# Cosformer attention and a mixture of experts: scaling k by cos and v by tan, kv with t innermost, row writes on VectorE, expert weights later

## The chip, the cores and the metric

The kernel runs on one core of one Trainium2 chip. The time is device microseconds for one execution, the median of several runs. A core has TensorE (PE, matmuls; its weight loads are listed as PEld), VectorE (DVE), ScalarE (ACT), GpSimd (POOL) and SyncE (SP, which here only issues transfers). Sixteen DMA engines move data between HBM and the on-chip memories SBUF and PSUM. The profile is of one execution and is somewhat longer than the timed runs.

## The reference

Eight batches of eight heads, 576 tokens, head dimension 64, go through a linear attention with a cosine weighting; its output, 4608 rows of 512, goes to one of eight experts each (top 1).

```python
theta = np.pi / 2.0 * pos / S                       # S = 576
phi(x) = concat([relu(x) * cos(theta), relu(x) * sin(theta)], -1)
kv  = einsum('bhsf,bhsd->bhfd', phi(k), v)          # f = 128, d = 64
z   = sum_s phi(k)
num = einsum('bhsf,bhfd->bhsd', phi(q), kv)
den = einsum('bhsf,bhf->bhs', phi(q), z) + 1e-06
x   = (num / den) as 4608 rows of 512
# experts
logits = x @ w_gate                                 # 8 experts
e = argmax(logits); g = softmax(logits)[e]          # denominator + 1e-9
# a token keeps its place if its expert has fewer than 1152 tokens before it
out[i] = g[i] * (relu(x[i] @ w1[e]) @ w2[e])        # 512 -> 1024 -> 512
```

The kernel never builds phi(q). Because sin = cos * tan, the query side is num = relu(q) kv_cos + tan * relu(q) kv_sin, and the common factor cos of a row falls out between num and den (den's 1e-6 is divided by cos for it).

## The kernel before

A list of operations is written with a cost, a priority and what it reads and writes; a small scheduler in the kernel file orders them on the host, and each engine then runs its instructions in that order. Tiles come from rings ("slots"): `p` and `a` are PSUM buffers (three and two), the rest lies in SBUF.

Attention of one batch `b`. The two halves `u` are four heads each; `j` counts nine tokens per partition, `t` is cos or sin:

```python
kS, vS, qS = Slots("km", 4), Slots("vm", 2), Slots("qm", 2)
vsS, rqS, kvaS = Slots("vs", 2), Slots("rq", 2), Slots("kva", 2)
tmpS = Slots("tmp", 3)

def relu_k(u):                                     # ACT; DVE for b == 0
    nc.scalar.activation(out=kk, in_=kk, func=ACT.Relu)        # 128 x 1152
def scale_v(j, t, us):                             # j odd or 4: ACT, else DVE
    tab = (cosn, sinn)[t]
    dst, src = vs_t[vs.slot][:, heads, j, t, 0:D], vm.tile[:, heads, j, :]
    # ACT: activation(Copy, scale=tab[:, j:j+1]);  DVE: tensor_scalar(mult)
# ...
def kv_half(u):                                    # PE: per j, c, o
    nc.tensor.matmul(out=kv_v[c * D:(c + 1) * D, o, u, :, :],
                     lhsT=loaded[b, "k", u].tile[o * D:(o + 1) * D, c, j, :],
                     rhs=vs_t[vs.slot][o * D:(o + 1) * D, 2 * u + c, j, :, :], ...)
def kvt_out():   # ACT copy of kv without z, to be transposed for the gate logits
def kva_out():   # ACT copy of kv with z
# T: four transposes of kvt; G: times w_gate; g_out: logits columns beside kv in kva

def p_unit(c, u, pv, tmp):                         # ten units a batch
    # PE:  p = relu(q)^T (as weights) x kva, cos and sin part side by side
    # ACT: tmp = p[cos part]
    nc.scalar.copy(out=t[0:rows], in_=p_v[0:rows, :, 0:KW])
    # DVE: num = p[sin part] * tan + tmp
    nc.vector.scalar_tensor_tensor(out=num..., in0=p_v[0:rows, :, KW:2 * KW],
        scalar=tant[0:rows, c:c + 1], in1=tmp.tile[0:rows], op0=ALU.mult, op1=ALU.add)
```

Routing of a batch follows: a chain of small DVE instructions gives the expert, the gate and the place of each token. Then the rows are scaled, written as bf16 (`xg`, five pieces) and scattered to a DRAM buffer `xd` sorted by expert:

```python
ON_POOL = (1, 3)
def f_emit(c):
    eng = nc.gpsimd if c in ON_POOL else nc.vector
    eng.tensor_tensor(out=x[0:rows, c, 0:DT]..., in0=num.tile[0:rows, c, :, 0:D],
                      in1=rv["rden"][0:rows, c, :]...to_broadcast(...), op=ALU.mult)
def f_scat(c):                                     # GpSimd queue
    nc.gpsimd.indirect_dma_start(out=xd[:, :], ...)
```

After the rows of six batches are in `xd`, 43 blocks of 128 rows are fetched and go through the experts: transpose, `up` with w1 (two halves w1a and w1b), relu, transpose, `down` with w2, indirect store. All expert weights are loaded with a cast to bf16 on the GpSimd queue; w1a during attention, w1b and w2 after it:

```python
for e in range(E):
    w1_load(0, e, e + 0.1, ops_of("KV", 3 * e // 4))   # after KV of batch 0, 0, 1, 2, 3, 3, 4, 5
for e in range(E):
    w1_load(1, e, 50.0 + e, [swapped])                 # after attention
```

## Time and profile before

Three runs took 385.45, 386.87 and 390.52 us, median 386.87. The profiled execution spans 396.6 us at a mean granted TensorE clock of 0.932.

| engine | busy us | share of the span | instructions |
|---|---|---|---|
| PE (matmul) | 336.3 | 85% | 3368 |
| PEld (weight loads, beside PE) | 221.2 | 56% | 3368 |
| DVE | 210.2 | 53% | 584 |
| ACT | 188.9 | 48% | 403 |
| POOL | 154.3 | 39% | 214 |

Some groups that the change touches:

| line, operation | engine | count | mean ns |
|---|---|---|---|
| L419 relu of k, 128x1152 | ACT | 14 | 1169 |
| L433 scaling of v, 128x256 | ACT | 70 | 519 |
| L435 scaling of v, 128x256 | DVE | 56 | 340 |
| L516 and L521 copies of kv | ACT | 16 | 571 and 605 |
| L581 tmp, 128x292 | ACT | 64 | 403 |
| L586 num, 128x292 | DVE | 64 | 517 |
| L758 row write, 128x512 | DVE | 16 | 1115 |
| L758 row write, 128x512 | POOL | 16 | 1520 |

How the lines are read. "L586" is line 586 of the kernel. A group of instructions gives line, engine, operation, output and input names, count, then busy time in us and the mean ns of one, then the idle time of the engine just before them and what ended it. A stretch ("70.00:90.00 20.00, ...") gives its length, then the busy us of PE, PEld, DVE, ACT and POOL with counts, the granted clock, the mean share of the 16 DMA engines that was busy, and GB/s. The slices of the page are 40 equal parts of the span, each digit a busy share in tenths. In the chain of waits each piece is start us, length us, and the work or transfer that the end depended on there. In the order of instructions the bracket gives the idle time in front and who ended it. Matmuls of fp32 count twice.

### The profile page before, as it was taken

The page shows a single profiled execution, that of the slowest core. Times are in us where ns is not written, and L with a number is a line of the kernel's source. Part 1 is how long each engine was busy: PE and PEld are TensorE (multiplying, and loading weights), DVE is VectorE, ACT ScalarE, POOL GpSimd, SP SyncE. Part 2 cuts the span into 40 slices and gives each one's busy share as a digit, 9 for nine tenths or more (in the row PEclk, how much of TensorE's full clock was granted, in tenths as well). Part 3 has the DMA queues.
Part 4 walks back from the last instruction along what each step waited for, and adds up shares of the span by engine and source line. Part 5 has one row for each costly group of instructions (what it writes and reads, how often), then busy time and mean ns, then how long its engine had stood idle before and what let it go on. Part 6 is the DMA issues. An engine that isn't in the chain of part 4 may idle for free.

```text
span 396.6 us, 9673 instructions
## 1 busy us (share of the span) xinstructions
PE 336.3 (85%) x3368; PEld 221.2 (56%) x3368; DVE 210.2 (53%) x584; ACT 188.9 (48%) x403; POOL 154.3 (39%) x214
## 2 busy tenths in 40 slices
PE   6588698878897996788397787899999999999992
PEld 3477597757686875674254343455555544444440
DVE  6547878796867697878725333444333311222220
ACT  5576776777675695547063232345555311111110
POOL 6100546454653627084723222105000065555552
PEclk9978986999797799989879998999999999999998
DMA  8999787778979501126599997819920033342330
GB/s 271 335 341 311 246 248 225 240 223 260 259 221 229 197 3 62 45 71 147 172 202 236 202 213 146 176 47 165 211 51 2 1 134 159 139 162 110 126 129 1
DMA packets 38543, 66.63 MB, mean 168 GB/s; under 512 B 3903, under 2 KB 18655, under 8 KB 38498
## 3 DMA queue, kind: packets, MB, share of 16 engines
q0 software_dynamic: 18096, 31.00, 34.5%
q1 hardware_dynamic: 19250, 33.98, 26.1%
q10 hardware_dynamic: 1152, 1.05, 0.8%
q8 instruction: 29, 0.48, 0.5%
q14 instruction: 16, 0.13, 0.1%
HBM read 67.56 MB, written 17.06 MB: 213 GB/s over the span
## 4 chain that ended last, share of the span: by engine, by line
PE 44%; DVE 15%; DMA 12%; issue 11%; POOL 6%; ACT 5%; POOLq 2%; ACTq 2%; SPq 1%; DVEq 0%
PE p L999 17%; PE p L574 9%; PE p L1040 7%; POOL out_dram L1057 6%; DMA xr<-xd 5%; DMA vm<-in_v_dram 5%; PE a L1014 4%; DVE xg L758 4%; DVE num L586 3%; PE a L468 3%; DMA qm<-in_q_dram 2%; POOLq L1057 2%; ACT tmp L581 2%; PE a L976 2%; PE a L547 1%
## 5 line engine op out<-in xcount | busy, mean ns | idle before, releaser
L1006 ACT ACTIVATE h<-p 128x512 bf16<-128x512 f32 x86 | 51.3, 598 | 63.3 <-PE p L999 61.7
L1040 PE MATMUL p<-w,un 128*128 x344 | 74.6, 379 | 0.3 <-issue 0.3
L574 PE MATMUL p<-kva,rq 64*128 64x146 f32 x640 | 61.2, 345 | 13.9 <-DVE num L586 10.9
L1020 DVE COPY un<-a 128x512 bf16<-128x512 bf16 x86 | 36.0, 423 | 63.5 <-PE a L1014 63.3
L574 PEld LDWEIGHTS p<-kva,rq 64*128 64x128 f32 x640 | 53.1, 229 | 21.8 <-DVE num L586 14.5
L1040 PEld LDWEIGHTS <-un 128*128 128x128 bf16 x344 | 33.6, 98 | 40.6 <-issue 0.6
L586 DVE SCALAR_TENSOR_TENSOR num<-p,tant,tmp 128x292 f32<-128x292 f32 (+1 forms) x80 | 39.8, 516 | 24.4 <-ACT tmp L581 19.2
L767 POOL DMA_INDIRECT xd<-xg,si x40 | 47.1, 1178 | 11.1 <-issue 8.8
L999 PEld LDWEIGHTS <-un 128*128 128x128 bf16 x344 | 32.7, 99 | 30.5 <-issue 9.5
L999 PE MATMUL p<-w1a,un 128*128 x172 | 46.7, 399 | 2.5 <-POOL ids L971 0.5
L581 ACT COPY tmp<-p 128x292 f32<-128x292 f32 (+1 forms) x80 | 31.2, 402 | 35.3 <-PE p L574 25.8
L1048 DVE COPY y<-p 128x512 f32<-128x512 f32 x22 | 15.2, 691 | 57.7 <-PE p L1040 51.9
L999 PE MATMUL p<-w1b,un 128*128 x172 | 44.1, 378 | 0.0
L1057 POOL DMA_INDIRECT out_dram<-y,ids x20 | 19.5, 976 | 58.5 <-DVE y L1048 46.8
L504 PE MATMUL p<-vs,km 64*64 64x130 f32 x1152 | 34.6, 272 | 9.1 <-DVE km L421 4.3
L1046 ACT COPY y<-p 128x512 f32<-128x512 f32 x21 | 12.3, 586 | 61.2 <-PE p L1040 61.2
L504 PEld LDWEIGHTS p<-vs,km 64*64 64x64 f32 x1152 | 32.1, 133 | 11.2 <-issue 5.2
L1014 PEld LDWEIGHTS <-h 128*128 128x128 bf16 x344 | 25.2, 99 | 22.5 <-ACT h L1006 10.0
L1014 PE MATMUL a<-identb,h 128*128 128x128 bf16 x344 | 33.5, 222 | 4.9 <-ACT h L1006 4.2
L758 POOL TENSOR_TENSOR xg<-num,rden 128x512 bf16<-128x512 f32 x16 | 24.0, 1520 | 18.4 <-DVE rden L735 18.4
L971 POOL COPY ids<-xr 128x2 bf16<-128x2 bf16 x43 | 7.6, 190 | 56.6 <-DMA xr<-xd 56.3
L468 PE MATMUL a<-ident,qr 128*128 128x128 f32 x144 | 27.3, 319 | 2.1 <-ACT rq L475 1.8
(162 smaller groups left out, 405.2 us busy)
## 6 DMA issues: line engine op xcount, KB each, us to landing
vm<-in_v_dram SPq DMA_DIRECT2D x16, 576.0 KB
km<-in_k_dram SPq DMA_DIRECT2D x16, 576.0 KB
qm<-in_q_dram SPq DMA_DIRECT2D x16, 576.0 KB
w<-in_moe_w_dram POOLq DMA_DIRECT2D x16, 512.0 KB
xr<-xd SPq DMA_DIRECT2D x43, 128.5 KB
w1a<-in_moe_w_dram POOLq DMA_DIRECT2D x8, 512.0 KB
w1b<-in_moe_w_dram POOLq DMA_DIRECT2D x8, 512.0 KB
xd<-zrow ACTq DMA_DIRECT2D x8, 128.5 KB
```

Source lines behind the costliest of these rows:

```text
L468: nc.tensor.transpose(out=q_ps[:, n * P:(n + 1) * P], in_=qr.tile[:, j, :, :].rearrange("p c d -> p (c d)"), identity=ident[:])
L504: nc.tensor.matmul(out=kv_v[c * D:(c + 1) * D, o, u, :, :], lhsT=loaded[b, "k", u].tile[o * D:(o + 1) * D, c, j, :], rhs=vs_t[vs.slot][o * ...
L574: nc.tensor.matmul(out=p_ps[:, a, o, 0:2 * KW], lhsT=rq[u].tile[a * D:(a + 1) * D, o, col:col + P], rhs=kva.tile[a * D:(a + 1) * D, o, u, ...
L581: nc.scalar.copy(out=t[0:rows], in_=p_v[0:rows, :, 0:KW])
L586: nc.vector.scalar_tensor_tensor(out=num.tile[0:rows, c, u * HB:(u + 1) * HB, :], in0=p_v[0:rows, :, KW:2 * KW], scalar=tant[0:rows, c:c + ...
L758: eng.tensor_tensor(out=x[0:rows, c, 0:DT].rearrange("p (h d) -> p h d", h=H), in0=num.tile[0:rows, c, :, 0:D], in1=rv["rden"][0:rows, c, ...
L767: si = nc.gpsimd.indirect_dma_start(out=xd[:, :], out_offset=bass.IndirectOffsetOnAxis(ap=xg.si[0:rows, c:c + 1], axis=0), in_=xg.tile[0:r ...
L999: nc.tensor.matmul(out=hp, lhsT=xv.tile[:, g, :], rhs=w1h[m][:, bass.ds(e1, 1), g, :], start=(g == 0), stop=(g == G - 1))
L1006: nc.scalar.activation(out=h[:], in_=pvs[m].tile[:, 0, :].rearrange("p (g q i) -> p g i q", g=2, i=2), func=ACT.Relu)
L1014: nc.tensor.transpose(out=t_ps[:, x * P:(x + 1) * P], in_=hvs[m].tile[:, x // 2, x % 2, :], identity=identb[:])
L1040: nc.tensor.matmul(out=y_ps, lhsT=hts[x // G].tile[:, x % G, :], rhs=w2h[x // G][:, bass.ds(e2, 1), x % G, :], start=(x == 0), stop=(x == ...
L1057: oi = nc.gpsimd.indirect_dma_start(out=out[:, :], out_offset=bass.IndirectOffsetOnAxis(ap=idx, axis=0), in_=yv.tile[:], in_offset=None, b ...
```

## The change

- The scalings change sides. k becomes relu(k)*cos in one instruction per j, and v*tan is added beside the untouched v, so that a KV matmul with relu(k)*cos on the left has v (cos part) and v*tan (sin part) on the right. v and v*tan of a slot lie in one tile and are joined by one operand with a stride between two runs of 66 elements. The `vs` tiles and the relu of k alone go away.
- kv is stored with t innermost (cos and sin of an element side by side), so one copy serves both the transposes and the p matmuls; kvt goes away. p comes out with t innermost too, and tmp and num read every second element.
- Row writes go to VectorE alone, in the order of the pieces. In routing the product for the gate logits is written with heads innermost and summed contiguously; the 1e-9 of the softmax is a ninth column, which takes an instruction on GpSimd away.
- w1a is loaded after KV of batches 4 to 7 (two loads each).
- Many evacuations may go to ACT or DVE, as the scheduler finds free; priorities (PHI) and ring sizes are set anew: km 2 slots of a whole batch, qm 4, rq 3, tmp 4.

It is meant to take work off ACT and DVE in attention, to keep GpSimd and VectorE out of each other's way, and to leave the first microseconds of DMA to q, k and v.

```diff
-    kS, vS, qS = Slots("km", 4), Slots("vm", 2), Slots("qm", 2)
-    vsS, rqS, kvaS = Slots("vs", 2), Slots("rq", 2), Slots("kva", 2)
-    tmpS = Slots("tmp", 3)
+    kS, vS, qS = Slots("km", 2), Slots("vm", 2), Slots("qm", 4)
+    rqS, kvaS = Slots("rq", 3), Slots("kva", 2)
+    tmpS = Slots("tmp", 4)
# ... scalings
+        def scale_k(j, us):
+            def f(eng):
+                kk = km.tile[:, 2 * us[0]:2 * us[-1] + 2, j, :]
+                if eng == "ACT":
+                    nc.scalar.activation(out=kk, in_=kk, func=ACT.Relu, scale=cosn[:, j:j + 1])
+                else:
+                    nc.vector.tensor_scalar(out=kk, in0=kk, scalar1=0.0, scalar2=cosn[:, j:j + 1], op0=ALU.max,
+                                            op1=ALU.mult)
+        def scale_v(j, us):
+            def f(eng):
+                dst, src = v_tan(vm.slot)[:, heads, j, 0:D], v_raw(vm.slot)[:, heads, j * D:(j + 1) * D]
+                # ACT: activation(Copy, scale=tann[:, j:j+1]);  DVE: tensor_scalar(mult)
# ... KV: columns 0:66 of v at (h, j) and of v*tan at (h, j)
+                            both = bass.AP(first.tensor, first.offset, [tuple(first.ap[0]), (v1 - v0, 2), (1, VX)])
+                            nc.tensor.matmul(out=kv_v[c * D:(c + 1) * D, 2 * o + u, :, :],
+                                             lhsT=km.tile[rows, 2 * u + c, j, :], rhs=both,
# ... one copy of kv, t innermost
+            t = tl(kva, [P, 4, KW, 2], FP32, "early")
+            copy(out=t[:, :, 0:D, :].rearrange("p w d t -> p w t d"), in_=kv_tile()[:, :, :, 0:D])
+            copy(out=t[:, :, D, :], in_=kv_tile()[:, :, 1, D:D + 2])
# ... evacuation of p
-                nc.scalar.copy(out=t[0:rows], in_=p_v[0:rows, :, 0:KW])
+                (nc.scalar.copy if eng == "ACT" else nc.vector.tensor_copy)(out=t[0:rows], in_=by_t(0))
-                    ... in0=p_v[0:rows, :, KW:2 * KW],
+                    ... in0=by_t(1),
# ... row writes
-                eng = nc.gpsimd if c in ON_POOL else nc.vector
-                eng.tensor_tensor(
+                nc.vector.tensor_tensor(
# ... weights
-        w1_load(0, e, e + 0.1, ops_of("KV", 3 * e // 4))
+        w1_load(0, e, e + 0.1, ops_of("KV", min(4 + e // 2, B - 1)))
```

Cut here: the scheduler's part that lets an operation choose between two engines, the set-up of the tables (tan on all partitions, the spread of w_gate on VectorE), and the same choice of engine for rq, tsb, gout, xT, relu, hT and y.

## The prediction

> **What bounds the kernel now.** I read the forty slices of the page first, for stages; then the busy times stretch by stage; then the chain of waits in order of time; then the instructions in order of time of one attention batch; last the groups of instructions by line and shape, for the durations used below.

> ```profile
> PE   6588698878897996788397787899999999999992
> DVE  6547878796867697878725333444333311222220
> ACT  5576776777675695547063232345555311111110
> DMA  8999787778979501126599997819920033342330
> ...
> 70.00:90.00 20.00, 16.25 (x283) 13.59 (x279) 16.46 (x43) 15.03 (x36) 10.55 (x10) 1.00 0.76 225
> 180.00:200.00 20.00, 12.78 (x94) 7.13 (x94) 15.68 (x53) 9.13 (x19) 12.08 (x20) 0.89 0.66 160
> 200.00:220.00 20.00, 17.82 (x142) 10.59 (x140) 7.99 (x21) 8.61 (x16) 5.10 (x13) 0.93 1.16 229
> 265.00:314.00 49.00, 48.70 (x349) 27.16 (x347) 19.13 (x47) 25.50 (x43) 5.63 (x8) 1.00 0.47 87
> ```

> A slice is 9.9 us. Three stages show. Attention runs to about 178 us: PE, DVE and ACT are each seven to nine tenths busy and none is full (70 to 90 us: PE 16.3, DVE 16.5, ACT 15.0 of 20 us at full clock), so the order and the waits between them set the pace. From 178 to about 250 us the experts start while DMA is full (1.16 from 200 to 220 us). From 265 us on PE is full (48.7 of 49) up to the last blocks; nothing on ACT or DVE can shorten that.

> ```profile
> 11.99 18.04 DMA vm<-in_v_dram
> ...
> 84.04 2.99 DVE xg L758 x2
> 87.03 0.67 DVE qr L458
> 87.97 1.30 DVE num L586 x3
> ...
> 85.50 1.53 DVE L758 TENSOR_TENSOR xg<-num,rden 64x512 bf16<-64x512 f32 x1
> 86.96 0.74 DVE L458 TENSOR_SCALAR qr<-qm 128x1152 f32<-128x1152 f32 x1
> 88.45 3.09 PE L574 MATMUL p<-kva,rq 64*128 64x146 f32 x40 [1.81 <-DVE num L586]
> 91.27 1.16 ACT L419 ACTIVATE km<-km 128x1152 f32<-128x1152 f32 x1
> 91.84 0.34 DVE L435 TENSOR_SCALAR vs<-vm,sinn 128x256 f32<-128x256 f32 x1
> 95.62 4.24 PE L504 MATMUL p<-vs,km 64*64 64x130 f32 x144 [1.17 <-DVE num L586]
> ```

> The first three pieces are the chain; the second group is the order of instructions. The product p (8 matmul passes a unit, ten units a batch, three PSUM buffers) is freed by a copy on ACT and a multiply-add on DVE (num). DVE comes late to it, behind the row writes xg and the relu of q, so PE waits 1.81 us; then ACT puts a 1.16 us relu of k and DVE several scalings between the evacuations. The 18 us on vm say that the head waits for loads.

> ```profile
> L758 POOL TENSOR_TENSOR xg<-num,rden 128x512 bf16<-128x512 f32 x16 | 24.0, 1520 | 18.4 <-DVE rden L735 18.4
> L758 DVE TENSOR_TENSOR xg<-num,rden 128x512 bf16<-128x512 f32 x16 | 17.2, 1115 | 0.3
> L758 DVE TENSOR_TENSOR xg<-num,rden 64x512 bf16<-64x512 f32 x8 | 12.2, 1529 | 0.0
> L419 ACT ACTIVATE km<-km 128x1152 f32<-128x1152 f32 x14 | 16.4, 1169 | 0.9 <-DMA km<-in_k_dram 0.9
> L433 ACT ACTIVATE vs<-vm,cosn 128x256 f32<-128x256 f32 x35 | 18.2, 520 | 1.9 <-DMA vm<-in_v_dram 1.9
> ```

> A row write on DVE takes 1.53 us beside one on POOL; the shortest of this line took 0.69.

> [...]the head shows a DMA share of 1.01 over its first 31 us. [...]the reads of p with t innermost (8 bytes apart) could cost more; no trace before has such an access on this shape.

> **The change, part by part.** Durations are of the groups by shape, unless said.

> *Scalings.* Before, a batch has 18 scalings of v (10 on ACT at 0.52, 8 on DVE at 0.34) and two relus of k on ACT at 1.17: ACT 7.5, DVE 2.7 us. After, it has 9 of k and 9 of v; by the order of the built kernel about 15 go to ACT and 3 to DVE in a steady batch: ACT 15 x 0.52 = 7.9, DVE 3 x 0.34 = 1.0. DVE gains 1.7 us a batch, ACT loses 0.4. The copy kvt (0.57) goes, a short second copy of kva (my guess 0.25, near the 0.27 of the 128-element rq copy) comes. ACT stays about level, in shorter pieces.

> *Row writes.* DVE before: 3.60 us a batch (three writes, in the order of time). After: 5 x 0.69 = 3.45. DVE keeps its time, POOL loses 2 x 1.52 = 3.0 us, which was off the path.

> *Routing.* The sum over heads reads contiguously (0.75 us before) but the product writes with a stride (0.49 before); I take a gain and a loss of 0.2, sum zero. The GpSimd step for the gate (0.25) goes.

> *kv with t innermost.* KV moves 132 columns for 130: 4.24 x 2/130 = 0.07 us a batch. The evacuations of p keep their element count, 0.40 and 0.52, if the stride is free.

> *Order.* This is the main term. In the new order DVE runs the ten num of a batch back to back, and ACT has one scaling of k after every third copy and the other seven after the last. The stretch from the first p to the next KV was 10.3 us (mean of 65.74 to 76.07, 84.88 to 95.62, 106.69 to 116.56, 129.43 to 139.41, 148.23 to 158.97). Its PE work is ten units at 0.587 (three units without a wait take 1.76) = 5.9 us, plus about 1.2 for q transposes, so 3.2 us is waiting. In the new order the units are paced by the slowest of PE 0.59, ACT (10 x 0.40 + 4 x 0.40)/10 = 0.56 (scalings follow each other at 0.40 in the order of time), DVE 0.52; with hand-overs I take 0.65, so 6.5 + 1.2 = 7.7. Gain 2.6 us. The other half of a batch, from KV to the first p, also 10.3 on average, hardly changes: DVE's way from the last num to the next (routing 3.4, relus of q 1.5, slots 1.3, row writes 3.45, scalings 0.7 = 10.4 us) is as long as the 10.6 measured from 57.0 to 67.6 us. Taking off 0.3 for hold-ups in the loads (below), a batch gains 2.3 us. KV of batches 1 and 7 start at 35.57 and 158.97, six periods of 20.6; six times 2.3 is 13.8 us.

> *Weights w1 late.* Two of eight w1a loads went out at 9.9 us. A weight load costs about 2.9 us of DMA, an estimate from 265 to 314 us (share 0.47 x 49 = 23 us for 8 loads). Without them the data of batches 1 and 2 land nearly 6 us earlier; DVE stops for vm for 3.0 us at 30.1, and PE 2.93 behind it. P of batch 0 took from 21.3 to 34.8 us where 7 to 8 us would do. I count 6 us for KV of batch 1.

> *Experts.* Total PE work is the same. Two w1b loads instead of one stand before the last scatters, in a stretch where DMA has room (0.66 from 180 to 200 us): one load, 2.9 us, of which I count half, 1.5.

> Sum: 13.8 + 6 + 1.5 = 21.3 us of the profiled 396.6; the timed runs are 386.87/396.6 = 0.975 of it, so 20.8. **Predicted: 366 us.**

> **Rivals.** (1) Loads become the bound. k and v of batch b+2 wait for KV of b; 2.36 MB at the head's 319 GB/s is 7.4 us, and k is wanted by ACT in the middle of P of b, some 13 us after KV's start, 9 after its end. With two w1a loads (5.8 us) sent at the same moment in batches 4 and 5, ACT would stop in front of the copies of p. For: KV frees both tiles at once[...]. Against: DMA share is 0.24 from 130 to 150 us, so the late weights have room. It would take back 3 to 8 us: 370 to 374. (2) Strides cost. If the two evacuations grow by 30%, num becomes 0.68 and tmp 0.52, ACT some 17 us a batch and P is back near 9.5: gain about 1 us a batch, 375 to 379. [...](3) The last two w1a loads, after KV of batch 7, arrive after the first expert matmul wants them. They have about 15 us (KV ended at 163.2, first up at 178.8) for 5.8 us of transfer; unlikely, 3 to 6 us. (4) Better: with the waits gone the batch falls to PE's 16 us, six times 4.5 = 27 us, and the experts' wait for rows shrinks too: 350 to 355.

> **Range and chances.** The main sum and rival 1 are likeliest, rivals 2 and 4 bound it: 353 to 378 holds it 8 times in 10. Two per cent is 7.7 us, 379.1; nearly all ways lie below: faster 0.87, within 0.09, slower 0.04.

> **What would show it.** KV of batch 7 starting near 139 instead of 159 us, KV of batch 1 near 29.5; a period near 18.3; P stretches under 8 us with few waits of PE on num; row writes of 0.69 on DVE and none on POOL; no wait of DVE on vm in the head; and the time from the first expert matmul to the end about 2 us less than 218. Wrong would be: tmp or num longer than 0.45 and 0.57 us (rival 2), ACT idle before scalings of k on its loads (rival 1), PE idle on w1a at the start of the experts (rival 3), or a period above 20 us.

## The result, and the profile after

The changed kernel takes 363.34 us (median of 4 runs, 362.18 to 366.79) against 387.21 us before (4 runs): ratio 0.939, 95% interval 0.930 to 0.948. A second measurement, beside later experiments, gave 0.938 (0.933 to 0.944). Here and below medians are over all runs, and ratios leave disturbed runs out. The prediction was 366, range 353 to 378.

The profile of before spans 396.6 us, that of after 360.4: 36 us apart, where the timed medians are 24 apart. So the kernel before was profiled once more (first experiment); that profile spans 383.2 us, near the timed runs, and is the one to set beside the profile after.

The forty slices after, the rows shown of before and PEclk:

```profile
PE   5779798999989998883998889999999999999991
DVE  5777889888898888787374435443333000000000
ACT  3588898989698754643444444555554333333330
PEclk9899899999999899996899999999999999999997
DMA  4999939596995768599999996499100244342230
```

A slice is now 9.0 us. PE is at eight or nine tenths from the sixth slice to the last but one, but for slice 19, which has 3 at a clock of 6. In attention DVE and ACT are at eight to nine for much of the time as well. All told DVE is busy for 187.3 us (210.2 before), ACT for 202.5 (188.9) and GpSimd for 126.9 (154.3): VectorE and GpSimd have less work, ACT has more. The stretches, in the columns described above:

```profile
70.00:90.00 20.00, 18.89 (x336) 15.94 (x328) 17.96 (x52) 18.60 (x49) 7.20 (x7) 1.00 0.81 255
160.00:180.00 20.00, 12.26 (x79) 6.99 (x78) 12.36 (x38) 7.55 (x14) 9.56 (x16) 0.74 1.12 224
180.00:200.00 20.00, 17.85 (x150) 10.86 (x151) 11.72 (x30) 8.73 (x15) 5.55 (x16) 1.00 1.13 218
200.00:220.00 20.00, 17.25 (x133) 9.67 (x134) 8.44 (x27) 9.04 (x16) 4.87 (x15) 1.00 0.98 192
240.00:290.00 50.00, 49.35 (x319) 26.48 (x323) 15.12 (x35) 23.70 (x40) 5.02 (x5) 1.00 0.36 79
```

From 70 to 90 us PE is busy for 18.9 us of 20 (16.3 before), ACT 18.6, DVE 18.0: three engines near full at once. From 160 to 180 us PE is down to 12.3 at a clock of 0.74: a new hole, taken up below. The long last stage is PE-bound as before (PE busy for 49.4 of 50 us).

The chain of waits after, two longest pieces of the head and the longest of batches 4 to 6:

```profile
8.09 12.73 DMA v<-in_v_dram
20.84 12.42 DMA km<-in_k_dram
...
98.25 6.82 DMA w1a<-in_moe_w_dram
```

The head still waits for loads, but ends sooner. The third piece, a late weight load, cost nothing that the trace shows: the chain goes from it to an instruction of VectorE (L752) that began 0.08 us after the end of the one in front of it, and the second profile of after has no such piece. The order of instructions in one steady batch:

```profile
73.08 3.09 DVE L786 TENSOR_TENSOR xg<-num,rden 128x512 bf16<-128x512 f32 x5
...
75.50 6.34 PE L603 MATMUL p<-kva,rq 64*128 64x146 f32 x80
...
76.37 1.40 ACT L613 COPY tmp<-p 64x292 f32<-64x292 f32 x3 [0.18 <-ACT rq L500]
76.80 1.52 DVE L617 SCALAR_TENSOR_TENSOR num<-p,tant,tmp 64x292 f32<-64x292 f32 x3
...
79.48 0.51 ACT L452 ACTIVATE km<-km,cosn 128x256 f32<-128x256 f32 x1
80.06 1.40 ACT L613 COPY tmp<-p 128x292 f32<-128x292 f32 x3
80.50 1.52 DVE L617 SCALAR_TENSOR_TENSOR num<-p,tant,tmp 128x292 f32<-128x292 f32 x3 [0.37 <-ACT tmp L613]
```

All 80 matmuls of p (40 in the program, each recorded twice) run in one piece of 6.34 us, with no wait inside; five row writes take 3.09 us. The groups by shape, with the durations that the prediction had used:

```profile
L603 PE MATMUL p<-kva,rq 64*128 64x146 f32 x640 | 51.7, 305 | 2.3 <-DVE num L617 0.6 <-ACT kva L579 0.3 <-ACT rq L500 0.2
...
L617 DVE SCALAR_TENSOR_TENSOR num<-p,tant,tmp 128x292 f32<-128x292 f32 x64 | 32.2, 520 | 9.7 <-ACT tmp L613 9.4
L613 ACT COPY tmp<-p 128x292 f32<-128x292 f32 x63 | 25.3, 402 | 9.4 <-PE p L603 4.7 <-DVE num L617 0.9
L452 ACT ACTIVATE km<-km,cosn 128x256 f32<-128x256 f32 x58 | 25.0, 499 | 1.2 <-DMA km<-in_k_dram 1.2
...
L786 DVE TENSOR_TENSOR xg<-num,rden 128x512 bf16<-128x512 f32 x32 | 20.1, 685 | 0.6
```

PE's wait for num fell from 10.9 to 0.6 us (12.2 and 0.4 in the second profiles of the two kernels). num and tmp with t innermost take 520 and 402 ns (517 and 403 before): the stride costs nothing here. KV, with 132 columns for 130, takes 4.29 us (4.24 before). A row write takes 685 ns, and each begins 0.60 us after the one in front of it.

### The profile page after: what moved, and what is told of

Read it like the earlier page. It is cut to its first block, busy times and chain, and to the rows that moved or that the text cites. A ratio compares the mean times of both kernels' runs of the same rounds, so it can differ in the third digit from the quotient of the medians.

```text
span 360.4 us, 9576 instructions
## 1 busy us (share of the span) xinstructions
PE 317.5 (88%) x3344; PEld 208.9 (58%) x3368; DVE 187.3 (52%) x546; ACT 202.5 (56%) x450; POOL 126.9 (35%) x189
## 4 chain that ended last, share of the span: by engine, by line
PE 43%; DMA 16%; ACT 10%; DVE 10%; issue 9%; POOL 7%; SPq 2%; ACTq 1%; POOLq 1%; DVEq 0%
PE p L1023 18%; PE p L1067 10%; PE p L603 7%; POOL out_dram L1081 6%; DMA xr<-xd 6%; PE a L1041 5%; DMA v<-in_v_dram 4%; DMA km<-in_k_dram 3%; ACT km L452 3%; DVE num L617 3%; DVE xg L786 2%; ACT v L463 2%; DMA w1a<-in_moe_w_dram 2%; PE a L1003 2%; DMA xd<-zrow 1%
## 5 line engine op out<-in xcount | busy, mean ns | idle before, releaser
L1032 ACT ACTIVATE h<-p 128x512 bf16<-128x512 f32 x65 | 38.9, 598 | 35.0 <-PE p L1023 32.2
L603 PE MATMUL p<-kva,rq 64*128 64x146 f32 x640 | 51.7, 305 | 2.3 <-DVE num L617 0.6
L1072 ACT COPY y<-p 128x512 f32<-128x512 f32 x42 | 24.6, 585 | 48.0 <-PE p L1067 46.9
L1047 DVE COPY un<-a 128x512 bf16<-128x512 bf16 x66 | 27.9, 423 | 43.0 <-PE a L1041 42.9
L603 PEld LDWEIGHTS p<-kva,rq 64*128 64x128 f32 x640 | 44.8, 196 | 8.3 <-DVE num L617 4.6
L1023 PE MATMUL p<-w1a,un 128*128 x162 | 43.8, 390 | 2.9 <-issue 1.4
L617 DVE SCALAR_TENSOR_TENSOR num<-p,tant,tmp 128x292 f32<-128x292 f32 (+1 forms) x80 | 39.9, 519 | 11.3 <-ACT tmp L613 10.7
L535 PE MATMUL p<-v,km 64*64 64x132 f32 x1152 | 36.0, 279 | 5.7 <-DMA v<-in_v_dram 4.8
L535 PEld LDWEIGHTS p<-v,km 64*64 64x64 f32 x1152 | 33.8, 136 | 7.9 <-issue 7.5
L613 ACT COPY tmp<-p 128x292 f32<-128x292 f32 (+1 forms) x77 | 30.8, 401 | 12.8 <-PE p L603 7.4
L452 ACT ACTIVATE km<-km,cosn 128x256 f32<-128x256 f32 (+1 forms) x67 | 27.9, 485 | 1.9 <-DMA km<-in_k_dram 1.9
L1081 POOL DMA_INDIRECT out_dram<-y,ix x23 | 22.3, 972 | 16.9 <-ACT y L1072 16.9
```

The costliest lines, as they stand in the source:

```text
L452: nc.scalar.activation(out=kk, in_=kk, func=ACT.Relu, scale=cosn[:, j:j + 1])
L535: nc.tensor.matmul(out=kv_v[c * D:(c + 1) * D, 2 * o + u, :, :], lhsT=km.tile[rows, 2 * u + c, j, :], rhs=both, start=(j == 0), stop=(j == ...
L603: nc.tensor.matmul(out=p_ps[:, a, o, 0:2 * KW], lhsT=rq[u].tile[a * D:(a + 1) * D, o, col:col + P], rhs=kva.tile[a * D:(a + 1) * D, 2 * o ...
L613: (nc.scalar.copy if eng == "ACT" else nc.vector.tensor_copy)(out=t[0:rows], in_=by_t(0))
L617: nc.vector.scalar_tensor_tensor(out=num.tile[0:rows, c, u * HB:(u + 1) * HB, :], in0=by_t(1), scalar=tant[0:rows, c:c + 1], in1=tmp.tile[ ...
L1023: nc.tensor.matmul(out=hp, lhsT=xv.tile[:, g, :], rhs=w1h[m][:, bass.ds(e1, 1), g, :], start=(g == 0), stop=(g == G - 1))
```

## The experiments

Twelve runs on three chips, here A, B and C. The kernel before took 398.5 us on A, 386.5 on B and 386.8 on C, so ratios to it are compared, not times; the last column is the ratio times 386.8. None of the runs on A and B is the changed kernel itself. One program, pads_on_sync, came to 0.933 on A and to 0.941 on C; so a difference between ratios of two chips may be wrong by 0.008, which is 3 us.

| run | chip | median us | ratio (95% interval) | x 386.8 |
|---|---|---|---|---|
| before_again | B | 385.2 (one) | | |
| after_again | C | 363.0 | 0.938 (0.933 to 0.944) | 363.0 |
| w1_early_again | A | 380.0 | 0.952 (0.946 to 0.957) | 368.1 |
| before_w1_late | B | 388.2 | 1.006 (1.003 to 1.009) | 389.0 |
| rows_on_pool_again | A | 376.8 | 0.946 (0.943 to 0.949) | 365.9 |
| before_rows_dve | B | 379.9 | 0.983 (0.974 to 0.991) | 380.1 |
| old_priorities | A | 396.0 | (0.994 of the medians) | |
| relu_apart | B | 387.9 | 1.006 (1.003 to 1.010) | 389.2 |
| kv_copied_twice | C | 372.7 | 0.958 (0.949 to 0.967) | 370.5 |
| stall_filled | C | 361.8 | 0.935 (0.930 to 0.940) | 361.6 |
| pads_on_sync | A | 372.4 | 0.933 (0.929 to 0.937) | 360.8 |
| pads_on_sync_2 | C | 364.5 | 0.941 (0.935 to 0.947) | 364.1 |

**before_again.** No edit.

> The kernel before, unchanged, for a second profile beside its first (which spanned 396.6 us at a mean clock of 0.932, with several waits behind PE at 0.74 to 0.84). If the clock made the first profile long, this one spans 385 to 390 us with a clock near 0.96, KV of batch 7 starts at 152 to 156 instead of 159, and the stretch from KV to the first p is near 9.5 us instead of 10.3. If not, it is near 396 again.

It spans 383.2 us, with KV of batch 7 at 150.22: even earlier than expected, at a clock of 0.944, lower than expected. The first profile had PE at half clock for 41 us between 14 and 180 us, the second for 31 (how this is counted stands below); and its stretches from the first p to the next KV took 9.9 to 10.7 us where the second has 8.3 to 8.8 in five of six. The first profile overstated what there was to gain there. With the second one the gain splits so:

| stage | predicted gain | before, second profile | after | gain |
|---|---|---|---|---|
| start to KV of batch 1 | 6 | 36.32 | 31.18 | 5.1 |
| KV of batch 1 to KV of batch 7 | 13.8 | 113.90 | 101.73 | 12.2 |
| KV of batch 7 to first expert matmul | 0 | 18.10 | 18.18 | -0.1 |
| first expert matmul to end | 1.5 | 214.88 | 209.29 | 5.6 |
| span | 21.3 | 383.2 | 360.4 | 22.8 |

Single profiles differ by some us in each row: with the second profile of after (next run) the five gains are 3.6, 14.2, -0.7, 5.7 and 22.7.

**after_again.** No edit, the control for chip C.

> The changed kernel unchanged, beside the next three on the same chip. Expected: ratio to the kernel before 0.935 to 0.945, and a profile with 4 to 6 periods of half clock before 180 us.

As expected: spans 360.5 us, KV of batch 7 at 132.47, five periods of half clock between 14 and 180 us.

**w1_early_again.** The loads of w1a go back to their old places in GpSimd's queue:

```diff
     plan.schedule()
+    # eight w1a loads: two ahead of the first scatter of batch 0, one behind its last, then behind or
+    # ahead of scatters of batches 1 to 4, as in the kernel before; the rest keeps its order
+    place([(0, ("scat", 0, 0)), (0, ("scat", 0, 0)), (1, ("scat", 0, 4)), (1, ("scat", 1, 4)), ...])
     plan.emit()
```

> The changed kernel with one thing undone: the eight w1a loads stand in the GpSimd queue where the kernel before had them (two after the rows of batch 0 are asked for, and so on); the order on every other engine is kept. Theory (the head waits for DMA, and an early w1a load delays k and v of batches 1 and 2): KV of batch 1 moves from 31.2 us back towards 35, and the whole takes 4 to 6 us more than the changed kernel's 363.3, 367 to 369, ratio to before about 0.952. Rival A (DMA catches up, the head's loss is made good in later batches): KV of batch 1 late, KV of batch 7 at 133 as before, time within 1 us of 363. Rival B (the late loads hurt batches 5 and 6, whose periods were 17.0 and 17.6 against 15.9): those two periods fall to 16 and 3 us of the loss come back, 365.

The ratio is 0.952 against 0.938 for the changed kernel on C: 5.1 us, the intervals do not touch. Against pads_on_sync, which ran on the same chip A, it is 7.3 us. KV of batch 1 starts at 39.37, against 32.6 for two other kernels of the same chip (rows_on_pool_again 32.55, pads_on_sync 32.65), and KV of batch 7 is 6 to 9 us behind them. Its chain of waits names what the head waits for:

```profile
4.40 4.92 DMA km<-in_k_dram
9.34 18.30 DMA km<-in_k_dram
```

So the head's term holds, in cause and, within the 3 us between chips, in size. Periods 5 to 6 and 6 to 7 were 19.95 and 18.13 us here, no shorter than the others: rival B did not show.

**before_w1_late.** The same part alone, on the kernel before (the loads stand where the changed kernel has them, by the same kind of edit).

> The kernel before with one part of the change: the w1a loads stand where the changed kernel has them, after KV of batches 4 to 7; order of every other engine kept. Theory: KV of batch 1 starts 4 to 6 us sooner and the gain stays to the end: 381 to 383 us, ratio about 0.987. Rival A: the head is made good anyway by later slack, ratio 1.00. Rival B: the late loads collide with k and v, or come too late for the experts: ratio above 1.00.

KV of batch 1 came at 29.17 us, 7.2 earlier than in before_again, as the theory says. Yet the time did not fall; it rose by 0.6%. KV of batch 7 was only 3.7 us ahead; one period took 25.06 us. In it, in order of time:

```profile
105.03 0.83 POOL L918 DMA_DIRECT2D w1a<-in_moe_w_dram  x1
...
115.01 0.24 POOL L749 TENSOR_SCALAR xg<-tok_i 128x5 int32<-128x5 int32 x1 [9.15 <-DMA xd<-xg,si]
115.34 0.23 POOL L667 TENSOR_SCALAR gate<-gate 128x5 f32<-128x5 f32 x1
...
115.60 0.19 DVE L670 RECIPROCAL gate<-gate 128x5 f32<-128x5 f32 x1 [7.18 <-POOL gate L667]
...
116.92 1.11 PE L468 MATMUL a<-ident,qr 128*128 128x128 f32 x4 [4.89 <-DVE pos L714]
```

GpSimd issues the w1a loads and the scatters of rows in one order. It waits 9.15 us until a scatter has landed and its `xg` buffer is free; behind that, in the same queue, stands the quarter microsecond that adds 1e-9 to the softmax sum; VectorE's reciprocal waits 7.18 us for it, and PE 4.89 for VectorE. The changed kernel has no such step (the ninth column does it on the way), so GpSimd's waiting stays GpSimd's. All told VectorE waited for this one step 4.5 us in before_again and 14.2 us here (14 to 170 us). So the late weights do not pay in the kernel before, and w1_early_again says that they pay in the changed one. That the ninth column makes the difference is read off these waits and was not tried: neither the ninth column alone nor the two together were put into the kernel before.

**rows_on_pool_again.**

```diff
-                nc.vector.tensor_tensor(
+                (nc.gpsimd if c0 in (1, 3) else nc.vector).tensor_tensor(
```

> The changed kernel with two of the five row writes of a batch on GpSimd again; order of all other instructions kept. Theory (VectorE's time for rows is the same either way, 3.60 against 3.45 us, so moving them is worth little): row writes of 1.5 us beside those on GpSimd come back, time 363 to 366, KV of batch 7 within 3 us of 132.9. Rival (VectorE's freedom from GpSimd's row writes is what brings the period down): 5 us or more, 368 and above, periods up by 1 us.

0.946 against 0.938 on C: 3 us, at the theory's upper edge, with intervals that just touch. Against pads_on_sync on the same chip it is 5 us, which is the rival's figure. So the writes are worth 3 to 5 us here, and the run does not decide between the two. The groups:

```profile
L786 POOL TENSOR_TENSOR xg<-num,rden 128x512 bf16<-128x512 f32 x16 | 20.4, 1275 | 69.6 <-DVE rden L764 69.4
...
L786 DVE TENSOR_TENSOR xg<-num,rden 128x512 bf16<-128x512 f32 x16 | 15.5, 1007 | 0.2
L483 DVE TENSOR_SCALAR qr<-qm 128x1152 f32<-128x1152 f32 x16 | 13.1, 818 | 1.5 <-DMA qm<-in_q_dram 1.3 <-issue 0.2
```

Row writes on VectorE are back at 1007 ns; three of them take 2.74 us, where five alone took 3.09. The mean of the relu of q, 818 ns for 745, comes from one of the sixteen: it took 1918 ns and is the only one that had a row write on GpSimd beside it, for 1095 ns of its time. The other fifteen took 735 to 760.

**before_rows_dve.**

```diff
-                eng = nc.gpsimd if c in ON_POOL else nc.vector
+                eng = nc.vector
```

> The kernel before with one part of the change: all five row writes of a batch on VectorE. Theory: VectorE has five writes of 0.69 us in place of three that took 3.6 us in all, so the time stays within 2 us: ratio 0.995 to 1.003. Rival[...]: VectorE's other work gets shorter beside it and the ratio is 0.985 or less.

0.983: 6.7 us, so the rival's figure. That VectorE's other work gets shorter is not seen: the relu of q is 756 ns either way. What got shorter are the row writes as a whole, and with them PE's wait for num. Batch 6, with the first 24 matmuls of p in 1.76 us in both (their time at full clock), first in before_again, then here:

```profile
139.97 3.60 DVE L758 TENSOR_TENSOR xg<-num,rden 128x512 bf16<-128x512 f32 x3
144.99 3.21 PE L574 MATMUL p<-kva,rq 64*128 64x146 f32 x42 [1.82 <-DVE num L586]
...
136.87 3.09 DVE L758 TENSOR_TENSOR xg<-num,rden 128x512 bf16<-128x512 f32 x5
141.38 2.84 PE L574 MATMUL p<-kva,rq 64*128 64x146 f32 x36 [1.31 <-DVE num L586]
```

Five writes on VectorE alone end 0.51 us sooner than three beside GpSimd's two, and PE waits 0.51 us less. The stretch from the first p to the next KV fell from 9.0 to 8.4 us on the mean of batches 1 to 6, which is 3.6 us in all. The chain through GpSimd got shorter too: its waits for the `xg` buffer went from 18.6 to 12.5 us, and VectorE's for the gate from 4.5 to 2.1. But the stretches from KV to the first p, in which these waits lie, took no less (10.0 and 10.2 on the mean). The two profiles are only 3.0 us apart, so what makes up the rest of the 6.7 is not shown.

**old_priorities.** The table PHI of the kernel before, with -0.73 for the new scalings; the same instructions, planned in another order.

> The changed kernel with the priority table of the kernel before (the new scalings get the priority that the old scalings had), so the same instructions in another order. Theory (the order, not the work taken off ACT and VectorE, is the main term of the gain): PE waits on num again, the period goes from 17.0 back to 19 to 20 us, the time to 371 to 378. Rival (the lower work and the shorter pieces on ACT and VectorE bring the gain in any order): period under 17.6, time 362 to 367.

Nearly the whole gain goes: 19 of 20 runs took 393.9 to 400.6 us and one 388.0, so no interval is given; the medians' ratio is 0.994. But not as the theory had it. KV of batch 7 came at 147.72, where two others of that chip, pads_on_sync and rows_on_pool_again, have 144.6 and 146.8; the six periods before it took 117.6 us, theirs 111.9 and 114.3. PE hardly waited for num. Its waits from 40 to 150 us:

```profile
PE a L559 <- DVE rq L500: 3.7, 1, 3.7
PE a L559 <- ACT rq L500: 3.0, 3, 1.3
PE a L573 <- ACT tsb L565: 2.1, 5, 0.5
PE p L603 <- DVE num L617: 1.0, 2, 0.7
```

The p stretches were short (6.3 to 8.2 us in batches 1 to 6, in those two 7.0 to 10.5), the halves before them long (9.8 to 16.7, against 8.6 to 11.0): PE waits for q and kv instead. Inside the p stretch the old table gives the order that the prediction describes, ten num in one run with a scaling after every third copy; so this run does not test that order, and what it changed lies in front of the stretch. And most of the loss lies behind attention: from the first expert matmul to the end 224.9 us, against 207.1 and 211.2 for those two. In this run the order at the experts cost more than that in attention; the prediction had taken it as given.

**relu_apart.**

```diff
                 kk = km.tile[:, 2 * us[0]:2 * us[-1] + 2, j, :]
+                if b and j in (0, 3):
+                    whole = km.tile[:, j // 3 * 2:j // 3 * 2 + 2, :, :]
+                    nc.scalar.activation(out=whole, in_=whole, func=ACT.Relu)
```

> The changed kernel with the folding of relu into the scaling of k undone: two more relus of k (128x1152 each, in place, some 1.17 us) on ACT in batches 1 to 7, in front of the scalings of j 0 and 3. 2.3 us more of ACT a batch. Theory (ACT is as near to being the bound as PE, and long pieces on it stand in front of the copies of p): nearly all of it shows, 1.5 to 2.3 us a batch, time 374 to 380. Rival (ACT has 3 us of slack a batch, what is folded away lay beside PE): 363 to 368.

26 us by the ratio (chip B against C), more than the 14 x 1.163 = 16.3 us of work that were added. Periods went from 16.6 (after_again) to 21.0 us. Clock can make up the rest: PE at half clock for 45.7 us between 14 and 180 us, in after_again 17.8; half of the difference, 14 us, is the most that it can cost by the estimate at the end. ACT has no slack in this order: work added to it cost 1.6 times its own length.

**kv_copied_twice.**

```diff
+            (nc.scalar.copy if eng == "ACT" else nc.vector.tensor_copy)(out=state["kvt"][:], in_=kv_tile()[:, :, :, 0:D])
             copy(out=t[:, :, 0:D, :].rearrange("p w d t -> p w t d"), in_=kv_tile()[:, :, :, 0:D])
```

> The changed kernel with a second copy of kv in front of the one that it has, on the same engine (the kernel before had two: kvt and kva). 0.6 us more on the way from KV to the transposes of kv in each batch. The prediction let the half of a batch from KV to the first p hang on VectorE's way (routing, relus of q, row writes) and gave the single copy no share of the gain. If that is right: within 1.5 us of the changed kernel. If the way over kv's copy, transposes and gate logits is what that half waits for: 7 batches x 0.6 = 4 us more, and up to twice that if PE's wait costs clock.

7.5 us by the ratio, intervals apart. Where both kernels run at full clock (batches 3 and 4) KV to first p takes 9.2 us for 8.9 and the period 16.2 for 15.9: 0.3 us of the 0.57 shows, 2.3 us in seven batches. Half clock rose from 17.8 to 29.4 us, which can cost 5.8 by the same estimate. That the way over kv's copy and VectorE's way are about equally long would explain the 0.3; that the second copy also fills ACT or VectorE was not kept apart from it. Clock can make up the larger part again.

**pads_on_sync and pads_on_sync_2.** The hole at 161 us after: PE waits 7.05 us for the copies of xT, which stand in ACT's queue behind eight transfers of zero rows that ACT issues from 158.85 to 167.3 us.

```diff
-                r0 = nc.values_load(T["end"][0:1, e:e + 1], engines=[ACTE], ...)
-                zi = nc.scalar.dma_start(out=xd[bass.ds(r0, P), :], in_=zrow[:])
+                r0 = nc.values_load(T["end"][0:1, e:e + 1], engines=[SP], ...)
+                zi = nc.sync.dma_start(out=xd[bass.ds(r0, P), :], in_=zrow[:])
```

> The changed kernel with the eight transfers of zero rows (the padding behind each expert's rows, issued by ACT from 158.9 to 167.3 us) issued by SyncE instead, between fetches of rows; order of all else kept. In the changed kernel PE stands still for 7.05 us there, behind the copies of xT on ACT. Theory: that stall is ACT's time as an issuer; PE goes on at 161, the clock stays up, and 4 to 6 us are gained: 357 to 360. Rival (DMA, at a share of 1.1 in that stretch, is the bound: PE then waits for w1b or rows instead, and what is gained is given back before 240 us): within 1 us of 363. Third way: SyncE is late with the fetches, since each transfer takes it about 1 us: 364 to 368.

> The changed kernel with the transfers of zero rows on SyncE, a second time, beside the changed kernel on the same chip. Theory (ACT's issuing is on the path from 159 to 167 us): 2 to 4 us less than the changed kernel, ratio between the two 0.990 to 0.994. Rival (the first measurement, 0.9327 of the kernel before, was that chip's share and no gain): within 1 us.

The first gave 0.933, which looked like a gain; the second, beside the changed kernel on one chip, 0.941 against 0.938: none is shown. Its instructions in order of time tell where it went:

```profile
171.33 1.28 DVE L1034 TENSOR_SCALAR h<-p 128x512 bf16<-128x512 f32 x2
172.07 1.44 PE L1023 MATMUL p<-w1a,un 128*128 x3 [3.95 <-DVE h L1034]
```

SyncE issues four of the eight transfers in 3.43 us, where ACT took 8.44 us for eight. With ACT free, PE waits 3.95 us for two relus that the plan, thinking ACT busy, had given to VectorE behind its table of blocks; and the half clock comes all the same (0.54 from 170 to 180 us). A plan made anew for this was not tried.

**stall_filled.** The hole stays, but PE does idle work in it:

```diff
                 hp = tl(pvs[m], [P, 2, 512], FP32, "ps")[:, 0, :]
+                if (i, m) == (6, 0):
+                    for _ in range(28):
+                        nc.tensor.matmul(out=hp, lhsT=zrow[:, 0:P], rhs=zrow[:, 0:512], start=True, stop=True)
```

> The changed kernel with 28 idle matmuls (zeros, 128x512 bf16, about 0.21 us each, 6 us in all) in front of the up matmuls of block 6, that is inside the 7 us for which PE otherwise stands still at 161 us. They compute nothing, and what waits for that block waits for VectorE until 168 us anyway. Over ten traces, a window of 3.41 us in which PE was idle for less than 0.4 us was never followed by half clock (0 of 208), one with 1.6 us or more nearly always (28 of 34). Theory (idle time itself takes the clock away): more work on PE makes the kernel faster; no half clock at 164 to 174, the ups after 168 take 1.0 us and not 1.9, 2 to 4 us are gained against the changed kernel. Rival (the clock falls for another reason, or the gain is given back to the loads): within 1 us of it, or slower by as much as the filling delays block 6.

In after_again:

```profile
160.00:170.00 10.00, 3.50 (x20) 1.91 (x18) 8.96 (x31) 2.86 (x6) 7.44 (x11) 0.75 1.08 244
170.00:180.00 10.00, 7.88 (x62) 4.84 (x62) 3.18 (x7) 4.69 (x9) 2.02 (x5) 0.91 1.10 200
```

With the filling, the same stretches:

```profile
160.00:170.00 10.00, 8.79 (x55) 4.41 (x53) 7.53 (x29) 4.59 (x9) 6.79 (x10) 1.00 1.07 225
170.00:180.00 10.00, 8.22 (x73) 5.29 (x75) 5.07 (x11) 4.11 (x8) 3.16 (x8) 1.00 1.16 221
```

And its order of instructions behind the hole:

```profile
168.32 1.02 PE L1026 MATMUL p<-w1a,un 128*128 x4
169.18 0.39 PE L1044 MATMUL a<-identb,h 128*128 128x128 bf16 x4
171.62 0.40 PE L1003 MATMUL a<-identb,xr 128*128 128x128 bf16 x4 [2.06 <-DMA xr<-xd]
```

The clock stays at 1.00 and an up takes 1.02 us, where after_again had 1.87 at 169.36; over six runs each, the mean clock was 0.965 to 0.982 against 0.954 to 0.970. So what the theory says of the clock is shown here. Its gain is not: 1.3 us by the medians, with intervals that overlap. From the first expert matmul to the end the two profiles take 209.7 and 209.2 us. PE waits for fetched rows 4.3 us at the experts, in after_again 3.3 (DMA share 1.11 and 1.09 from 160 to 180 us); where the rest of what the clock saved goes was not found. Of all versions run, this has the lowest median on a chip shared with the changed kernel, but it is not shown to beat it.

## Why the prediction was right, and where its steps were not

*The sum* was right in part by luck. Against the second profile of before, its terms come out so:

| term | predicted us | measured us |
|---|---|---|
| head | 6 | 5.1 |
| p stretch, six batches | 15.6 | 7.3 |
| KV to first p, six batches | 0 | 4.9 |
| hold-ups in the loads | -1.8 | in the two rows above |
| KV of batch 7 to the experts | 0 | -0.1 |
| experts | 1.5 | 5.6 |
| sum | 21.3 | 22.8 |

The head is right in cause and size. The largest term is half of what was written, and two rows for which nothing or little was counted made it good. KV of batch 7 came at 132.9 where "near 139" was written; but 159, from which it was counted, was 150 in the second profile.

*Period, p stretch (10.3 to 7.7).* The end was sized well: 7.0 us in three batches, 7.7 on the mean. The beginning was read off one profile that was slower than the timed runs; against the second (9.0 on the mean) the step is worth 1.2 us, not 2.6. That the new order does it is read off the lines above (80 matmuls in one piece, 0.6 us of waits for num) and was undone by no run; 0.5 us of the step comes with the row writes alone.

*Period, KV to first p ("hardly changes").* It fell from 10.0 to 9.2 us on the mean of batches 1 to 6. Undisturbed it did not: 8.7 before and 8.9 after. What went are the three long ones of before_again (10.7 to 12.3): in two of them PE ran partly at half clock (30.8 us of it in that profile between 14 and 180 us), and in the longest of these it also waited 2.5 us behind VectorE's wait for GpSimd's gate step; in the third it stood still for 1.9 us for a reason that the profile does not show. The two errors nearly cancel: 2.6 - 0.3 = 2.3 a period predicted, 2.0 measured.

*Row writes ("DVE keeps its time").* This step failed. 3.45 us was reckoned as five times 0.69, the author's estimate of an undisturbed write from the shortest one in the profile of before. With two of the five on GpSimd a write on VectorE takes 1115 ns on the mean in before and 1007 in rows_on_pool_again; with none there it takes 685 in after. But each write begins 0.60 us after the one in front of it, and five take 3.09; against 3.60 before, VectorE comes to num 0.51 us sooner in an undisturbed batch, not 0.15, and PE's wait for num shrinks by that. The whole is worth 6.7 us alone in the kernel before, and 3 to 5 in the changed one. *The GpSimd step for the gate*, for which the prediction counted nothing, hangs VectorE on GpSimd's queue and on the scatters' landing, as batch 5 of before_w1_late shows (7.18 us).

*Scalings.* Some 15 or 16 in a steady batch on ACT at 0.50 to 0.51 us, 7.6 us for 15 where 7.9 was written. That two relus of k more on ACT would cost more than their own time (relu_apart) was not foreseen.

*Experts (1.5).* Measured 5.6. In old_priorities the same instructions in another order took 14 to 18 us longer there; how much of the 5.6 is order, choice of engine or w1b was not taken apart.

*Rivals.* (1) is there and very small: scalings of k waited 1.0 and 0.7 us for their loads in the period of batch 5 (0.2 in after_again), and nothing of the kind shows in batches 2 to 4, 6 and 7. The periods of 17.0 and 17.6 us, where the three before took 15.9 to 16.3, are not its doing alone: stall_filled, with no such wait, has 16.9 and 16.5, and the 17.6 has a half-clock window in its p stretch (123.29 to 126.70 us; the 80 matmuls of p take 7.15 us for 6.34). (2) did not come: with t innermost the reads out of PSUM take 402 ns (tmp) and 520 (num), where 403 and 517 were measured before; that they could cost more was the author's conjecture. (3) did not come; the new wait at the experts' start was ACT's issuing. (4) came in half: in the middle batches the period is 15.9 to 16.3 us, in the others 17.0 to 19.1.

## What to carry to other kernels

Profile the kernel before twice and set the profiled span beside the timed median, before sizing a step from one trace. Follow short steps on a lightly used engine: what stands in front of them in that engine's queue (here a buffer that waits for a scatter) becomes the wait of a busy engine. Where writes follow each other on one engine, take their cost from start to start (0.60 us here), not from the length of one (0.69). And where three engines are near full, count what a delay can cost PE's clock, not only PE's waiting (here at most 6.5 to 7 us of 22.8, by the estimate below).

## What the runs showed of the hardware

| PE idle in the window, us of 3.41 | windows | followed by half clock |
|---|---|---|
| under 0.4 | 327 | 0 |
| 0.4 to 0.8 | 112 | 6 |
| 0.8 to 1.2 | 55 | 8 |
| 1.2 to 1.6 | 40 | 17 |
| 1.6 and more | 42 | 34 |

In stall_filled PE is busy for 8.79 of the 10 us from 160 to 170 us, 4 of them with work that computes nothing, where after_again has 3.50 in all; its clock stays at 1.00 to 180 us, where after_again has 0.75 from 160 to 170 and 0.91 from 170 to 180. So there it is PE's idleness that takes the clock away. Adding up 2 x (1 - clock) over windows of 1 us from 14 to 180 us gives the us of half clock used above:

| kernel | half clock, us | KV of batch 7 |
|---|---|---|
| before, first and second profile | 41.0 and 30.8 | 158.97 and 150.22 |
| after, first and second profile | 17.1 and 17.8 | 132.91 and 132.47 |
| kv_copied_twice | 29.4 | 140.10 |
| relu_apart | 45.7 | 160.54 |
| stall_filled | 5.7 | 130.55 |

Of the 12.1 us by which stall_filled has less than after_again, 6.8 stand behind the filled hole; the rest lies elsewhere and varies from run to run. In after four matmuls of an up take 1.02 us at full clock (156.35 us) and 1.86 at half (169.76 us). As an estimate from this, PE does at least half its work at half clock, so half of such a number is the most that it can lose: at most 6.5 to 7 us of the gain of 22.8 between the second profile of before and the first of after. Why chip A is slower (the same kernel with the transfers on SyncE spans 375.3 us there and 362.4 on C) stays open; the durations of single instructions on ACT and VectorE show no such difference (tmp 402 ns and num 520 in rows_on_pool_again on A, 401 and 519 in relu_apart on B).
